# Attention followed by a gated MLP in fp32: the gelu's denominator made as |h|·(b1·|h| + b0) with its product on GpSimd, in place of a square on ScalarE and a sum on VectorE

## Chip, cores and metric

One core of a Trainium2 chip. The metric is the device time of one execution in microseconds (us): 651.39 us, the median of three runs of the kernel before (651.1 to 655.28). Engines are named as in the profile: PE (TensorE matmul), PEld (TensorE weight load), DVE (VectorE), ACT (ScalarE), POOL (GpSimd), SP (SyncE, which here issues DMAs).

## The reference, cut to what matters

Local attention (4 batches, 8 heads, 768 positions, head size 64, a window of 16 keys to either side and 24 block summaries) makes `x` of 3072 tokens by 512. Then comes the part that the change touches:

```python
h = x @ w_in                      # 3072 x 2048
h2 = h * h
h3 = h2 * h
P = a[0] + a[1] * h + a[2] * h2 + a[3] * h3
Q = 1.0 + np.abs(b[0]) * np.abs(h) + np.abs(b[1]) * h2
g = P / (Q + 1e-06)
return (g @ w_out).astype(np.float32)
```

All of it is fp32. The weights arrive as 8-byte floats. `Q` is the denominator of which the change speaks.

## The kernel before, in words

**Tiling.** The 3072 tokens are six groups of 512 (`GT`); the 2048 hidden columns are 16 tiles of 128 (`NFC`). One step is one group and one tile, so there are 96 steps, and the loop at L551 runs them in order, with `LAG` = 3 more turns for what trails. fp32 precision is kept by splitting each operand of a matmul into a high and a low part. In each step `moe1` (L390) makes `h`, 128x512, in PSUM from 12 matmuls (high·high, low·high, high·low, four chunks each), `gelu` (L402) turns `h` into `gh` and `gl`, and three steps later `moe2` (L432) adds 12 matmuls with `gh` and `gl` into four PSUM tiles `po`.

**The gelu** (L402 to L430) has these instructions for each step, all 128x512. ACT: a square, an absolute value with scale, a linear form `tu`. DVE: `tq` = square·b1 + |h|·b0 (L420). ACT: `ta` = exp(-ln(`tq` + 1)), the reciprocal. DVE: two products that finish the cubic `P` in `tu` (L407, L409), then `gh`, a remainder in `tq`, a remainder in `tu` (L426 to L428). POOL: `gl` = `tu`·`ta` (L430). `ta`, `tq` and `tu` have two buffers each, `h` two PSUM buffers, `gh` and `gl` three. The square goes either into `tq` itself, in SBUF, or into a PSUM tile `sq` of the pool `ps_a`, which attention uses too (L413 to L415). The first form is taken in steps 0, 1, 3, 4, 6, 7, 9 and 10, in later steps that start attention, and from the end of attention on; the second in the rest.

**What else runs.** Attention works in halves of 64 positions. A half's scores come from PE (`sc`); DVE adds the mask and takes the extreme (`ss`, a custom instruction, and `sm`); ACT makes the exponentials; DVE the reciprocal of their sum; POOL scales the four parts of `ss` (L245); then PE transposes (`pt`) and multiplies with the values (`av`). During the first 14 steps the weights are also split (`w_split`, L353): for each of the 16 tiles ACT scales the raw words `wr`, POOL makes integers of a byte of each (L369), DVE joins them (L372), ACT rounds the high part into `wearly` or `w` (L382) and DVE subtracts for the low part (L385).

**Order.** PE's order is that of the program text throughout. For the first 14 steps (`NSTRICT`) the orders of DVE, ACT and POOL are too: the string `STEP` (L56) lists what each step issues, `g0` being the next part of this step's gelu and `g1` that of the step before. After that the scheduler of the tile framework orders DVE, ACT and POOL by priority and by its own estimate of times. Every engine runs its queue in order, so an instruction that waits holds back all behind it on that engine.

The constants sit in `cs`: columns 4 and 5 hold |b0| and |b1| scaled by 2^-32, column 7 the scaled 1.000001.

Of the kernel before, what the change touches and what calls it, by code (L numbers as in the profile page):

```python
# [8 lines left out]
F32 = mybir.dt.float32  # L9
# [3 lines left out]
AF = mybir.ActivationFunctionType  # L13
ALU = mybir.AluOpType
# [8 lines left out]
P = 128  # L23
NPAIR = H // 2
NCC = DM // P
NFC = DFF // P
# [8 lines left out]
GT = 512  # L35
# [18 lines left out]
NSTRICT = NFC - 2  # L54
CROSS = 1
STEP = "h3 k0 h0 l0 h1 a0 w2 h1 g1 h3 h0 u w3 g0 w2 g0 q0 h0 w2 g1 w3 q0 P2 v h2 g0"  # L56
NHALF = NT // HQ
# [3 lines left out]
def tile_kernel(ctx, tc, qw_in, kraw, kwin, vpad, vred, wio, a, b, cmask, cident, cavg, out):  # L61
# [12 lines left out]
    ps_a = ctx.enter_context(tc.tile_pool(name="ps_a", bufs=2, space=PSUM))  # L74
# [23 lines left out]
    pe, dve, act, gps = Kept(nc.tensor), Kept(nc.vector), Kept(nc.scalar), Kept(nc.gpsimd)  # L98
# [6 lines left out]
    cs = const.tile([P, 8], F32, name="cs")  # L105
# [13 lines left out]
    def setup():  # L119
        nc.scalar.dma_start(out=mask, in_=cmask)  # L120
        nc.scalar.dma_start(out=ident, in_=cident)
        nc.scalar.dma_start(out=coef[:, 0:4], in_=a)
        nc.scalar.dma_start(out=coef[:, 4:6], in_=b)
        dve.tensor_scalar_mul(cs[:, 0:6], coef, SH)
        dve.tensor_scalar_mul(cs[:, 6:7], cs[:, 5:6], -1.0)
        dve.tensor_tensor(cs[:, 5:6], cs[:, 5:6], cs[:, 6:7], op=ALU.max)
        dve.memset(cs[:, 7:8], C1 * SH)

    ksum, vsum, att, x32, prods = {}, {}, {}, {}, {}
# [272 lines left out]
    def gelu(h, gh, gl, g, fc):  # L402
        ta = mp.tile([P, GT], F32, tag="ta", name=f"ta{g}_{fc}")
        tq = mp.tile([P, GT], F32, tag="tq", name=f"tq{g}_{fc}")
        tu = mp.tile([P, GT], F32, tag="tu", name=f"tu{g}_{fc}")
        def products():
            dve.tensor_tensor(tu, tu, h, op=ALU.mult)  # L407
            yield
            dve.scalar_tensor_tensor(out=tu, in0=tu, scalar=cs[:, 1:2], in1=h, op0=ALU.add, op1=ALU.mult)  # L409


        prods[g * NFC + fc] = products()
        sq = tq  # L413
        if g * NFC + fc < start_of(NHALF - 1) + 4 and ((g * NFC + fc) not in halves if g * NFC + fc > NSTRICT else g * NFC + fc in (2,5,8,11,12,13,)):
            sq = ps_a.tile([P, GT], F32, tag="a", name=f"sq{g}_{fc}")  # L415
        act.activation(sq, h, AF.Square)
        act.activation(ta, h, AF.Abs, scale=cs[:, 4:5])
        act.activation(tu, h, AF.Identity, scale=cs[:, 3:4], bias=cs[:, 2:3])
        yield
        dve.scalar_tensor_tensor(out=tq, in0=sq, scalar=cs[:, 5:6], in1=ta, op0=ALU.mult, op1=ALU.add)  # L420
        yield
        act.activation(ta, tq, AF.Ln, bias=cs[:, 7:8])
        act.activation(ta, ta, AF.Exp, scale=-1.0)
        yield
        lead(prods.pop(g * NFC + fc), True)
        dve.scalar_tensor_tensor(out=gh, in0=tu, scalar=cs[:, 0:1], in1=ta, op0=ALU.add, op1=ALU.mult)  # L426
        dve.scalar_tensor_tensor(out=tq, in0=tq, scalar=C1 * SH, in1=gh, op0=ALU.add, op1=ALU.mult)
        dve.scalar_tensor_tensor(out=tu, in0=tu, scalar=cs[:, 0:1], in1=tq, op0=ALU.add, op1=ALU.subtract)  # L428
        yield
        gps.tensor_tensor(gl, tu, ta, op=ALU.mult)  # L430
# [62 lines left out]
    def lead(chain, all_of=False):  # L493
        for _ in chain or ():
            if not all_of:
                return
# [37 lines left out]
    def start_of(jj):  # L534
        return EARLY_HALF[jj - HPG] if jj < 2 * HPG else NFC - 2 - (jj >= 3 * HPG) + 4 * ((jj - 2 * HPG) // 2)

    halves = {}
# [13 lines left out]
    for step in range(NG * NFC + LAG):  # L551
        g, fc = divmod(step, NFC)
# [133 lines left out]
```

## Time and profile before

| what | value |
|---|---|
| time, median of 3 runs | 651.39 us (651.1 to 655.28) |
| profiled execution, first to last instruction (span) | 647.9 us |
| busy: PE, DVE, ACT, POOL | 96%, 89%, 71%, 40% of the span |
| POOL `gl`, 96 instructions, mean | 1345 ns |
| POOL waited for DVE's `tu` | 159.6 us |
| ACT waited for DVE's `tq` | 74.7 us |

The page gives the profiled execution's span and no time of its own beside it; the median of the runs is 3.49 us above the span, for what lies before the first and after the last instruction. A row of a group reads: line, engine, operation, output<-inputs, shapes, count, then busy us and mean ns of one, then the idle time before. Every line is L88 here because one helper records all operations, so groups are told apart by tile names. In a table of windows each engine has its busy us and the number of its instructions. A row of a timeline has start, duration, engine, instruction, count, and in brackets the idle time before it with what ended it.

### The profile page before, as it was taken

Reading aid. Unit: us, or ns where it says so; the run is one execution under the profiler, and the core shown is the slowest. Engines: PE = TensorE matmul, PEld = TensorE weight load, DVE = VectorE, ACT = ScalarE, POOL = GpSimd, SP = SyncE. Lnnn points to the kernel's source line nnn. Section 1 sums busy time; section 2 is a strip of 40 time slices with the busy share of each in tenths; the row PEclk is TensorE's granted clock in tenths of the full one; section 3 lists DMA queues with packets and bytes.
Section 4 is the critical chain, followed back from the end, with each engine's and each line's share of the span. In section 5 each row is a group of like instructions: output and inputs, shape, how many; then the busy total and the mean of one; then the engine's idle time right before and its main releaser. Section 6 shows DMA issues by size and latency. Waiting matters only on the chain.

```text
span 647.9 us, 11828 instructions
## 1 busy us (share of the span) xinstructions
PE 624.7 (96%) x4068; PEld 499.4 (77%) x4068; DVE 576.9 (89%) x1152; ACT 459.0 (71%) x1032; POOL 257.4 (40%) x350
## 2 busy tenths in 40 slices
PE   8998879988999999999999999999999999999997
PEld 5666657866788887788888778888788888888886
DVE  4699999999998989988999999988988888988885
ACT  3889869977677577767758677758767756765652
POOL 1855666754243235244233244333334232222221
PEclk9999979989999999999999999999999999999999
DMA  9997644403354435234424332314233110010001
GB/s 322 340 356 263 205 148 157 139 26 107 113 176 116 125 122 160 83 128 150 119 88 141 103 129 93 108 63 130 66 129 114 40 64 1 21 45 1 0 2 65
DMA packets 51559, 77.00 MB, mean 119 GB/s; under 512 B 6068, under 2 KB 33076, under 8 KB 49580
## 3 DMA queue, kind: packets, MB, share of 16 engines
q1 hardware_dynamic: 50796, 75.80, 36.1%
q8 instruction: 32, 0.52, 0.3%
q10 hardware_dynamic: 576, 0.25, 0.1%
q0 software_dynamic: 128, 0.20, 0.1%
q14 instruction: 27, 0.22, 0.1%
HBM read 61.31 MB, written 14.73 MB: 117 GB/s over the span
## 4 chain that ended last, share of the span: by engine, by line
PE 51%; DVE 29%; ACT 7%; issue 6%; POOL 6%; DMA 1%; SPq 0%; DVEq 0%; POOLq 0%
PE po L88 24%; PE h L88 22%; DVE tu L88 10%; DVE tq L88 7%; DVE gh L88 4%; POOL ss L88 4%; ACT ss L88 3%; PE av L88 2%; DVE xl L88 2%; PE sc L88 2%; ACT ta L88 2%; DVE ss L88 2%; DVE ks L88 1%; DMA kres<-in_kraw_dram 1%; PE pt L88 1%
## 5 line engine op out<-in xcount | busy, mean ns | idle before, releaser
L88 POOL TENSOR_TENSOR gl<-tu,ta 128x512 fp32r<-128x512 f32 x96 | 129.1, 1345 | 298.9 <-DVE tu L88 159.6
L88 POOL TENSOR_SCALAR ss<-ss,sm 128x120 f32<-128x120 f32 x192 | 95.2, 513 | 81.6 <-DVE sm L88 79.5
L88 ACT ACTIVATE ta<-tq,cs 128x512 f32<-128x512 f32 x96 | 69.7, 726 | 76.3 <-DVE tq L88 74.7
L88 PE MATMUL po<-wearly,gh 128*128 128x512 f32 x384 | 122.8, 401 | 0.0
L88 PE MATMUL po<-w,gh 128*128 128x512 f32 x384 | 121.7, 398 | 0.0
L88 PE MATMUL h<-xh,wearly 128*128 128x512 f32 x384 | 96.1, 392 | 1.6 <-DVE sm L88 1.1
L88 PE MATMUL h<-xh,w 128*128 128x512 f32 x384 | 95.0, 389 | 0.0
L88 PEld LDWEIGHTS h<-xh,wearly 128*128 128x128 f32 x384 | 71.9, 188 | 18.7 <-ACT wr L88 1.3
L88 ACT ACTIVATE ss<-ss,sm 128x120 f32<-128x120 f32 x192 | 73.2, 384 | 15.4 <-DVE sm L88 15.2
L88 PEld LDWEIGHTS h<-xh,w 128*128 128x128 f32 x384 | 72.0, 188 | 15.2 <-ACT x L88 0.2
L88 PEld LDWEIGHTS po<-w,gh 128*128 128x128 f32 x384 | 71.3, 190 | 16.0 <-issue 1.7
L88 PEld LDWEIGHTS po<-wearly,gh 128*128 128x128 f32 x384 | 70.6, 191 | 16.2 <-issue 2.2
L88 DVE SCALAR_TENSOR_TENSOR gh<-tu,cs,ta 128x512 fp32r<-128x512 f32 x96 | 73.2, 762 | 9.2 <-ACT ta L88 1.2
L88 PE MATMUL po<-w,gl 128*128 128x512 f32 x192 | 75.4, 393 | 0.0
L88 PE MATMUL po<-wearly,gl 128*128 128x512 f32 x192 | 75.4, 393 | 0.0
L88 DVE SCALAR_TENSOR_TENSOR tu<-tu,cs,tq 128x512 f32<-128x512 f32 x96 | 72.9, 760 | 2.5
L88 ACT ACTIVATE tu<-h,cs 128x512 f32<-128x512 f32 x96 | 74.7, 778 | 0.0
L88 DVE SCALAR_TENSOR_TENSOR tu<-tu,cs,h 128x512 f32<-128x512 f32 x96 | 71.3, 743 | 2.3
L88 DVE SCALAR_TENSOR_TENSOR tq<-tq,gh 128x512 f32<-128x512 f32 x96 | 66.3, 691 | 3.0
L88 ACT ACTIVATE ta<-h,cs 128x512 f32<-128x512 f32 x96 | 65.2, 679 | 3.0 <-POOL gl L88 2.9
L88 DVE TENSOR_TENSOR tu<-tu,h 128x512 f32<-128x512 f32 x96 | 64.9, 676 | 0.0
L88 ACT ACTIVATE ta<-ta 128x512 f32<-128x512 f32 x96 | 60.9, 634 | 2.8
(73 smaller groups left out, 925.3 us busy)
## 6 DMA issues: line engine op xcount, KB each, us to landing
wr<-in_wio_dram SPq DMA_DIRECT2D x15, 1024.0 KB
cross<-tb SPq DMA_DIRECT2D x32, 256.0 KB
vw<-in_vpad_dram SPq DMA_DIRECT2D x42, 192.0 KB
kw<-in_kwin_dram SPq DMA_DIRECT2D x40, 192.0 KB
pts<-cross SPq DMA_DIRECT2D x96, 64.0 KB
out_dram<-o SPq DMA_DIRECT2D x24, 256.0 KB
qw<-in_qw_dram SPq DMA_DIRECT2D x40, 128.0 KB
kr<-in_kraw_dram SPq DMA_DIRECT2D x12, 384.0 KB
```

The source lines that it names most:

```text
L88: out = getattr(self.engine, name)(*args, **kw)
```

## The change

The denominator without its constant, b1·h² + b0·|h|, is computed as |h|·(b1·|h| + b0). ACT makes |h| without a scale into `ta`; ACT reads `ta` and makes b1·|h| + b0 into `tq`; POOL multiplies the two into `tq`. The square, the PSUM tile `sq` with its rule, and the DVE instruction go. In the set-up one DVE instruction makes |b0| and |b1| together, where two made |b1| alone.

```diff
-        dve.tensor_scalar_mul(cs[:, 6:7], cs[:, 5:6], -1.0)
-        dve.tensor_tensor(cs[:, 5:6], cs[:, 5:6], cs[:, 6:7], op=ALU.max)
+        dve.scalar_tensor_tensor(out=cs[:, 4:6], in0=cs[:, 4:6], scalar=-1.0, in1=cs[:, 4:6], op0=ALU.mult, op1=ALU.max)
...
         prods[g * NFC + fc] = products()
-        sq = tq
-        if g * NFC + fc < start_of(NHALF - 1) + 4 and ((g * NFC + fc) not in halves if g * NFC + fc > NSTRICT else g * NFC + fc in (2,5,8,11,12,13,)):
-            sq = ps_a.tile([P, GT], F32, tag="a", name=f"sq{g}_{fc}")
-        act.activation(sq, h, AF.Square)
-        act.activation(ta, h, AF.Abs, scale=cs[:, 4:5])
+        act.activation(ta, h, AF.Abs)
+        act.activation(tq, ta, AF.Identity, scale=cs[:, 5:6], bias=cs[:, 4:5])
         act.activation(tu, h, AF.Identity, scale=cs[:, 3:4], bias=cs[:, 2:3])
         yield
-        dve.scalar_tensor_tensor(out=tq, in0=sq, scalar=cs[:, 5:6], in1=ta, op0=ALU.mult, op1=ALU.add)
+        gps.tensor_tensor(tq, tq, ta, op=ALU.mult)
         yield
         act.activation(ta, tq, AF.Ln, bias=cs[:, 7:8])
         act.activation(ta, ta, AF.Exp, scale=-1.0)
```

How this moves instructions: PE's order is the same in both. DVE, ACT and POOL change in the three places below. In the rows a name such as `gl0_7` is `gl` of group 0, step 7, `ss13` is attention's half 13, `wr11` the raw weights of tile 11, and the number after the last underscore is an instance number of the listing.

POOL in steps 8 and 9 of the first group, where the text sets the order; before:

```order
L88 TENSOR_SCALAR ss13_1194<-ss13_1194,sm13_1195 128x120 x4
L88 TENSOR_TENSOR gl0_7_1160<-tu0_7_1203,ta0_7_1201 128x512
L88 TENSOR_SCALAR wr11_1030<-wr11_1030 128x1024
L88 TENSOR_TENSOR gl0_8_1249<-tu0_8_1262,ta0_8_1260 128x512
L88 TENSOR_SCALAR wr12_1216<-wr12_1216 128x1024
```

and with the change:

```order
L88 TENSOR_SCALAR ss13_1191<-ss13_1191,sm13_1192 128x120 x4
L88 TENSOR_TENSOR tq0_8_1258<-tq0_8_1258,ta0_8_1257 128x512
L88 TENSOR_TENSOR gl0_7_1157<-tu0_7_1200,ta0_7_1198 128x512
L88 TENSOR_SCALAR wr11_1027<-wr11_1027 128x1024
L88 TENSOR_TENSOR tq0_9_1343<-tq0_9_1343,ta0_9_1342 128x512
L88 TENSOR_TENSOR gl0_8_1246<-tu0_8_1259,ta0_8_1257 128x512
L88 TENSOR_SCALAR wr12_1213<-wr12_1213 128x1024
```

The new product of a step stands ahead of `gl` of the step before and of the weights' conversion `wr`.

DVE over the same stretch; before:

```order
L88 SCALAR_TENSOR_TENSOR gh0_7_1159<-tu0_7_1203,cs_95,ta0_7_1201 128x512
L88 SCALAR_TENSOR_TENSOR tq0_7_1202<-tq0_7_1202,gh0_7_1159 128x512
L88 SCALAR_TENSOR_TENSOR tu0_7_1203<-tu0_7_1203,cs_95,tq0_7_1202 128x512
L88 SCALAR_TENSOR_TENSOR tq0_8_1261<-sq0_8_1263,cs_95,ta0_8_1260 128x512
L88 TENSOR_TENSOR tu0_8_1262<-tu0_8_1262,h0_8_1235 128x512
L88 TENSOR_TENSOR w10_1267<-wr10_975,w10_1267 128x1024
L88 SCALAR_TENSOR_TENSOR tu0_8_1262<-tu0_8_1262,cs_95,h0_8_1235 128x512
L88 SCALAR_TENSOR_TENSOR wr11_1030<-wr11_1030 128x1024
```

and with the change:

```order
L88 SCALAR_TENSOR_TENSOR gh0_7_1156<-tu0_7_1200,cs_95,ta0_7_1198 128x512
L88 SCALAR_TENSOR_TENSOR tq0_7_1199<-tq0_7_1199,gh0_7_1156 128x512
L88 SCALAR_TENSOR_TENSOR tu0_7_1200<-tu0_7_1200,cs_95,tq0_7_1199 128x512
L88 TENSOR_TENSOR tu0_8_1259<-tu0_8_1259,h0_8_1232 128x512
L88 TENSOR_TENSOR w10_1263<-wr10_973,w10_1263 128x1024
L88 SCALAR_TENSOR_TENSOR tu0_8_1259<-tu0_8_1259,cs_95,h0_8_1232 128x512
L88 SCALAR_TENSOR_TENSOR wr11_1027<-wr11_1027 128x1024
```

One row is gone and nothing else moved; the last row needs POOL's `wr11`.

ACT in steps 7 and 8 of the second group, where the scheduler sets the order; before:

```order
L88 ACTIVATE sq1_7_2357<-h1_7_2339 128x512
L88 ACTIVATE ta1_7_2354<-h1_7_2339,cs_95 128x512
L88 ACTIVATE tu1_7_2356<-h1_7_2339,cs_95 128x512
L88 ACTIVATE ta1_7_2354<-tq1_7_2355,cs_95 128x512
L88 ACTIVATE ta1_7_2354<-ta1_7_2354 128x512
L88 ACTIVATE sq1_8_2418<-h1_8_2400 128x512
L88 ACTIVATE ta1_8_2415<-h1_8_2400,cs_95 128x512
```

and with the change:

```order
L88 ACTIVATE ta1_7_2341<-h1_7_2326 128x512
L88 ACTIVATE tu1_7_2343<-h1_7_2326,cs_95 128x512
L88 ACTIVATE tq1_7_2342<-ta1_7_2341,cs_95 128x512
L88 ACTIVATE ta1_8_2401<-h1_8_2386 128x512
L88 ACTIVATE tu1_8_2403<-h1_8_2386,cs_95 128x512
L88 ACTIVATE tq1_8_2402<-ta1_8_2401,cs_95 128x512
L88 ACTIVATE ta1_7_2341<-tq1_7_2342,cs_95 128x512
L88 ACTIVATE ta1_7_2341<-ta1_7_2341 128x512
```

The affine form now comes third, after `tu`, and here the logarithm of step 7 stands behind three instructions that need `h` of step 8.

## The prediction, made before the changed kernel was run

> **What bounds the kernel now.** I read the table of windows first, because the shares of the whole span mix two regimes.
>
> ```profile
> 37.00:135.00 98.00, 88.03 (x550) 66.47 (x551) 95.17 (x177) 86.50 (x178) 62.10 (x55) 0.96 0.58 193
> 135.00:183.00 48.00, 45.06 (x287) 35.78 (x287) 45.88 (x94) 34.77 (x84) 17.28 (x21) 0.98 0.32 98
> 183.00:530.00 347.00, 343.94 (x2266) 280.98 (x2265) 313.91 (x659) 247.23 (x579) 128.90 (x210) 1.00 0.36 111
> 530.00:633.00 103.00, 103.00 (x482) 85.14 (x481) 90.30 (x117) 63.53 (x102) 26.27 (x19) 1.00 0.03 11
> ```
>
> The columns after the window's length are PE, PEld, DVE, ACT and POOL busy, then the granted clock and DMA. From 183 to 633 us PE is busy for 446.94 of 450 us: DVE could be free there and little would change, since the most that can be won is 3 us. From 37 to 135 us it is otherwise: PE is busy for 88.03 of 98 us, DVE for 95.17. Here DVE sets the pace, and this is where the change can give or cost. The two rows of the same windows for the instructions on `h` alone count the steps: 156 matmuls, 13 steps of 12, in the first, and 84, seven steps, in the second.
>
> ```profile
> 37.00:135.00 98.00, 38.83 (x156) 29.06 (x156) 16.94 (x24) 23.08 (x38) 0.96 0.58 193
> 135.00:183.00 48.00, 20.75 (x84) 15.77 (x84) 9.92 (x14) 12.33 (x21) 0.98 0.32 98
> ```
>
> Next, one early step on POOL and on DVE, step 8 of group 0 (from one DVE `wr` to the next, 103.25 to 110.60, 7.35 us).
>
> ```profile
> 103.42 3.77 POOL L88 TENSOR_SCALAR ss<-ss,sm 128x120 f32<-128x120 f32 x4 [1.91 <-DVE sm L88]
> 107.16 1.30 POOL L88 TENSOR_TENSOR gl<-tu,ta 128x512 fp32r<-128x512 f32 x1
> 108.55 2.01 POOL L88 TENSOR_SCALAR wr<-wr 128x1024 int32<-128x1024 uint8 x1
> ...
> 103.25 1.19 DVE L88 SCALAR_TENSOR_TENSOR wr<-wr 128x1024 int32<-128x1024 int32 x1
> 104.36 0.74 DVE L88 SCALAR_TENSOR_TENSOR gh<-tu,cs,ta 128x512 fp32r<-128x512 f32 x1
> 105.14 0.69 DVE L88 SCALAR_TENSOR_TENSOR tq<-tq,gh 128x512 f32<-128x512 f32 x1
> 105.87 0.75 DVE L88 SCALAR_TENSOR_TENSOR tu<-tu,cs,tq 128x512 f32<-128x512 f32 x1
> 106.53 0.75 DVE L88 SCALAR_TENSOR_TENSOR tq<-sq,cs,ta 128x512 f32<-128x512 f32 x1
> 107.20 0.68 DVE L88 TENSOR_TENSOR tu<-tu,h 128x512 f32<-128x512 f32 x1
> 108.08 1.46 DVE L88 TENSOR_TENSOR w<-wr,w 128x1024 fp32r<-128x1024 f32 x1 [0.21 <-ACT w L88]
> 109.47 0.73 DVE L88 SCALAR_TENSOR_TENSOR tu<-tu,cs,h 128x512 f32<-128x512 f32 x1
> 110.60 1.23 DVE L88 SCALAR_TENSOR_TENSOR wr<-wr 128x1024 int32<-128x1024 int32 x1 [0.39 <-POOL wr L88]
> ```
>
> Two things are to be seen. The last row waits for POOL's `wr`: in this step POOL's queue, not DVE, ends the wait. And POOL is slow because it takes turns with DVE: its four small scalings need 3.77 us while DVE runs `wr`, `gh`, `tq`, `tu`, all with two inputs in SBUF, and POOL's `wr` takes 2.01 us, of which 1.02 come after DVE's `w` has ended at 109.54. Steps 9 and 10 end the other way round, with POOL ahead:
>
> ```profile
> 114.17 1.29 POOL L88 TENSOR_TENSOR gl<-tu,ta 128x512 fp32r<-128x512 f32 x1 [3.61 <-DVE tu L88]
> ...
> 114.72 1.29 DVE L88 SCALAR_TENSOR_TENSOR tq<-tq,cs,ta 128x512 f32<-128x512 f32 x1
> 115.94 0.68 DVE L88 TENSOR_TENSOR tu<-tu,h 128x512 f32<-128x512 f32 x1
> 118.74 1.19 DVE L88 SCALAR_TENSOR_TENSOR wr<-wr 128x1024 int32<-128x1024 int32 x1
> ```
>
> ```profile
> 118.92 3.76 POOL L88 TENSOR_SCALAR ss<-ss,sm 128x120 f32<-128x120 f32 x4 [1.91 <-PE sc L88]
> 122.65 1.29 POOL L88 TENSOR_TENSOR gl<-tu,ta 128x512 fp32r<-128x512 f32 x1
> 124.03 1.45 POOL L88 TENSOR_SCALAR wr<-wr 128x1024 int32<-128x1024 uint8 x1
> ...
> 122.83 1.65 DVE L88 SCALAR_TENSOR_TENSOR tq<-tq,cs,ta 128x512 f32<-128x512 f32 x1
> 124.41 0.68 DVE L88 TENSOR_TENSOR tu<-tu,h 128x512 f32<-128x512 f32 x1
> 127.22 1.19 DVE L88 SCALAR_TENSOR_TENSOR wr<-wr 128x1024 int32<-128x1024 int32 x1
> ```
>
> Step 9 has no scalings on POOL and takes 118.74 - 110.60 = 8.14 us; step 10 takes 127.22 - 118.74 = 8.48. In both the instruction that the change removes, `tq<-tq,cs,ta`, started while `gl` ran and took until `gl` was done.
>
> **The change part by part.** The groups give the prices.
>
> ```profile
> L88 POOL TENSOR_TENSOR gl<-tu,ta 128x512 fp32r<-128x512 f32 x96 | 129.1, 1345 | 298.9 <-DVE tu L88 159.6 <-ACT ta L88 70.3 <-DVE sm L88 27.2
> L88 DVE SCALAR_TENSOR_TENSOR tq<-tq,cs,ta 128x512 f32<-128x512 f32 x43 | 48.1, 1118 | 11.3 <-ACT ta L88 10.9
> L88 DVE SCALAR_TENSOR_TENSOR tq<-sq,cs,ta 128x512 f32<-128x512 f32 x53 | 39.1, 738 | 4.0 <-ACT ta L88 3.9
> L88 ACT ACTIVATE sq<-h 128x512 f32<-128x512 f32 x53 | 30.9, 583 | 27.3 <-PE h L88 27.3
> L88 ACT ACTIVATE ta<-tq,cs 128x512 f32<-128x512 f32 x96 | 69.7, 726 | 76.3 <-DVE tq L88 74.7
> L88 ACT ACTIVATE ta<-ta 128x512 f32<-128x512 f32 x96 | 60.9, 634 | 2.8
> ```
>
> Removed from DVE: 48.1 + 39.1 = 87.2 us. Added to POOL: 96 products of two SBUF operands of 128x512, the kind of `gl`, so 96 x 1.345 = 129 us. On ACT a 583 ns square becomes an affine form read from SBUF, between the 634 and the 726 ns of the two such rows: 5 to 14 us in all, hidden in ACT's 99.77 idle us of 183 to 530; in the early window 13 times 0.05 to 0.14 lie in 11.5 idle us. The set-up loses one small DVE instruction, and some DMA issues on SP move by a place or two; both I take as nothing, for the constants are made before the first `h`, and no row above waits for those transfers.
>
> The same DVE operation costs 738 ns with its first input in PSUM and 1118 ns with both in SBUF: 380 ns are waiting for POOL. The Trainium skill, page "SBUF — State Buffer", section "Who interferes with whom", says so as a rule: a DVE instruction with two SBUF inputs and a GpSimd instruction that reads SBUF exclude each other, and the second to issue is blocked until the first is done. The trace agrees in kind (the 1.65 us above), and the rule speaks against this change; what it would make of the sum is a rival below.
>
> *Steps 0 to 13.* Step 8 after the change: scalings done at 3.91 us (107.16 - 103.25), the new product 1.30, DVE's `w` in its turn 1.2, `gl` 1.30, `wr` 1.02, and only then DVE's next `wr`: 8.73 us instead of 7.35, +1.38. The cover that DVE gives up (0.75) is worth nothing here, because POOL's queue ends the step. Behind the product stand `gl` and `wr`, and DVE's `wr` and so `gh` wait for the latter. Step 9: DVE loses 1.22 (115.94 - 114.72); the product takes its turn once among `gh`, `tq`, `tu`, and holds one up by up to 1.30: +0.1. Step 10: the same POOL sum as step 8, 8.73, against 8.48: +0.25. Together +1.7 for three steps. The three kinds recur, so four rounds in steps 2 to 13: **+6.9 us**. Bounds: if DVE never waits for the new product, step 8 is 3.91 + 1.30 + 1.30 + 1.02 = 7.53 (+0.2), step 9 loses 1.2, step 10 is bound by the same 7.53 (-0.95): -1.95 a round, -7.8. If in every step the product comes on top with nothing in return, 1.35 to 1.38 each, 4.1 a round: +16.4. I take the value in between because the rows show turns being taken.
>
> *Steps 13 to 19, 135 to 183 us.* DVE is busy for 45.88 of 48 us, POOL for 17.28 only. Seven steps lose 0.74 each, -5.2. The three two-input instructions of a step (0.74, 0.69, 0.75) fill about a third of its 6.9 us, so I charge a third of 1.3 back, 0.4 each: **-2.4 us**, bounds -5.2 and, with 1.3 each, +3.9.
>
> *183 to 633 us.* What hides the longer way is the lag of three steps:
>
> ```profile
> 581.49 2.72 PE h L88 x12
> 600.52 2.72 PE po L88 x12
> 633.16 10.95 PE po L88 x48
> ...
> 590.58 1.29 POOL L88 TENSOR_TENSOR gl<-tu,ta 128x512 fp32r<-128x512 f32 x1 [4.50 <-DVE tu L88]
> 640.22 1.29 POOL L88 TENSOR_TENSOR gl<-tu,ta 128x512 fp32r<-128x512 f32 x1 [4.50 <-DVE tu L88]
> ```
>
> `h` of a step is done at 584.21, its `gl` at 591.87, and PE reads it from 600.52 on: 8.65 us to spare. The affine form behind `tu` (0.7), a product of 1.3 instead of 0.74, and `gl` behind the next step's product (1.3) use about 2.6 of it. **0 us**, bounds -3 (all of PE's idle time) and +8 (the ACT rival). Without that cover the 2.6 us would come in every step.
>
> *The end.* Only the last step has no cover: its `gl` ends at 641.51 and PE's last matmuls need it. One more 0.7 on ACT and 0.56 on POOL, against DVE's old wait for the `gl` before: **+0.2**, bounds 0 and 1.3.
>
> Sum: 6.9 - 2.4 + 0 + 0.2 = +4.7 us on the span of 647.9, so 652.6. The median of the runs, 651.39, is 3.49 above the span; the forecast is **656.1 us**, 0.7% slower, which a measurement of this kernel, good to about 1%, may not tell from no change.
>
> **The rivals.** *The freed DVE wins.* Two DVE waits go, 0.74 to 1.2 us a step, and no new ones come. For it: DVE is busy for 95.17 of 98 us. Against it: POOL ends step 8, and the new work stands in that very queue. By the lower bounds -7.8 - 5.2 = -13.0: 638.4 us. It would need steps 9 and 10 shorter by over 1 us each. Chance 0.12.
>
> *The shared port fills up, slower.* Place: steps 2 to 13, between POOL's product and DVE's `gh`, `tq`, `tu`, `w`. Price: each of the steps pays the product whole, +16.4 - 2.4 + 0.2: 665.6 us. It decides for "slower" as soon as steps 9 and 10 grow by over 0.5 each. For it: the 3.77 us of the scalings; against it: the removed SBUF form gives the port back 0.74 in two of three steps. Chance 0.26. This is the rule of the Trainium skill's page "SBUF — State Buffer" taken at its word, every overlap blocked for the whole instruction.
>
> *ACT's new order costs PE in the attention steps, slower.* In the order of the second group the logarithm of step 7 stands behind three instructions that wait for `h` of step 8, one PE step of 5.44 us (twice 2.72) later. With the 2.6 from above 0.6 of the 8.65 are left. If attention's work on ACT eats that and 0.5 us is lost in each of the 14 rounds of four steps (96 steps less the 20 counted above and the 19 that 103 us hold at 5.44), +7: 663.1 us. Against it: gaps of that kind would have to pass the two buffers of `ta` without the scheduler's other work filling them. Chance 0.14.
>
> *Within 1%*, the forecast, has 0.48. Faster by over 1% is the first rival, 0.12; slower by over 1% the two others, 0.40. The forecast's own range is 651 to 658. The range for 8 in 10 goes from 645, half of the first rival's gain, to 667, past the port rival.
>
> **What would show it.** Right: in step 8 and the two like it (three steps before and after) DVE's wait for POOL's `wr` grows from 0.39 to over 1 us, and those steps last 8.5 to 8.8; the new product takes about 1.3 us; from 37 to 135 us DVE's busy share falls while the work of that window takes 5 to 8 us longer; PE stays above 99% from about 190 us on. Wrong: the thirteenth step done earlier than before; `gh`, `tq` and `tu` keeping 0.69 to 0.75 while POOL's product runs; PE idle by more than 6 us in the attention steps after 190; or a product far from 1.3 us.

## The result, and the profile after

The changed kernel takes **687.02 us** (median of 4 runs, 686.13 to 690.64) against 651.77 us for the kernel before beside it: a ratio of 1.0556, 95% interval 1.0513 to 1.0599, 35 us slower. The forecast was 656.1 us, 0.7% slower, with a range from 645 to 667. The change is slower, and by more than any case of the prediction allowed (665.6 us at most). Of all runs of the kernel before, one took 693.0 us at a granted clock of 0.85, where every other run shows 0.93 or more; it is left out of the medians and ratios below.

First the same windows as in the prediction's table, up to 530 us (PE, PEld, DVE, ACT and POOL busy, granted clock, DMA):

```profile
37.00:135.00 98.00, 85.64 (x546) 65.05 (x546) 87.67 (x163) 84.96 (x171) 78.88 (x65) 0.97 0.57 191
135.00:183.00 48.00, 41.17 (x261) 30.73 (x260) 41.17 (x65) 32.18 (x65) 29.25 (x28) 0.96 0.23 69
183.00:530.00 347.00, 323.22 (x2101) 263.62 (x2098) 277.46 (x575) 234.67 (x555) 189.37 (x244) 0.99 0.35 109
```

The third row is the news: PE, which had been busy for 343.94 of 347 us, is idle there for 23.8. DVE, from which the work was taken, got emptier in every row, and PE did not gain from it in any.

The early steps look as they were forecast. POOL, then DVE, in the place that the prediction's step 8 had:

```profile
109.16 1.28 POOL L88 TENSOR_TENSOR tq<-tq,ta 128x512 f32<-128x512 f32 x1
110.41 2.27 POOL L88 TENSOR_TENSOR gl<-tu,ta 128x512 fp32r<-128x512 f32 x1
...
105.40 1.23 DVE L88 SCALAR_TENSOR_TENSOR wr<-wr 128x1024 int32<-128x1024 int32 x1 [0.30 <-POOL wr L88]
109.50 2.02 DVE L88 TENSOR_TENSOR w<-wr,w 128x1024 fp32r<-128x1024 f32 x1
113.91 1.23 DVE L88 SCALAR_TENSOR_TENSOR wr<-wr 128x1024 int32<-128x1024 int32 x1 [1.73 <-POOL wr L88]
121.96 1.23 DVE L88 SCALAR_TENSOR_TENSOR wr<-wr 128x1024 int32<-128x1024 int32 x1 [0.31 <-POOL wr L88]
```

From one DVE `wr` to the next, step 8 takes 113.91 - 105.40 = 8.51 us (7.35 before), and DVE's wait for POOL's `wr` has grown from 0.39 to 1.73; step 9 takes 8.05 (8.14). The steps like 8, three steps before and after it, take 8.46 and 8.52 us where they had 7.26 and 7.32. `gl` and `w` hold each other up: 2.27 us and 2.02 us, where they had 1.30 and 1.46.

The groups after show the product's price and what else became longer:

```profile
L88 POOL TENSOR_TENSOR tq<-tq,ta 128x512 f32<-128x512 f32 x96 | 129.2, 1346 | 125.3 <-ACT tq L88 125.0
L88 DVE SCALAR_TENSOR_TENSOR gh<-tu,cs,ta 128x512 fp32r<-128x512 f32 x96 | 91.0, 948 | 40.1 <-ACT ta L88 38.6 <-ACT tq L88 0.5
L88 DVE SCALAR_TENSOR_TENSOR tq<-tq,gh 128x512 f32<-128x512 f32 x96 | 78.4, 817 | 7.2
L88 ACT ACTIVATE tq<-ta,cs 128x512 f32<-128x512 f32 x96 | 77.9, 812 | 0.5
L88 ACT ACTIVATE ta<-h 128x512 f32<-128x512 f32 x96 | 57.0, 593 | 95.1 <-POOL gl L88 79.3 <-PE h L88 15.7
```

The product costs 1346 ns, as forecast. `gh` went from 762 to 948 ns and `tq<-tq,gh` from 691 to 817, without any edit to them. The last row is the one to remember: ACT's absolute value, the first instruction of a step's gelu, now waits 79.3 us for POOL's `gl`.

Who waits for whom from 183 to 530 us, before and then after (total us, times, longest):

```profile
ACT sq L88 <- PE h L88: 22.8, 26, 2.1
ACT tq L88 <- PE h L88: 13.6, 11, 2.1
PE av L88 <- DVE tu L88: 2.1, 4, 1.1
```

```profile
ACT ta L88 <- POOL gl L88: 54.4, 32, 4.6
ACT ta L88 <- POOL tq L88: 38.0, 28, 4.1
DVE tu L88 <- ACT tu L88: 24.1, 15, 3.2
PE av L88 <- DVE tu L88: 21.8, 13, 3.8
```

Before, ACT came to a new step early and waited for PE's `h` (22.8 + 13.6 us). After, ACT waits for POOL, DVE waits for ACT, and PE waits for DVE: 21.8 of PE's 23.8 idle us stand in one row. One such place after, and the same place before:

```profile
457.03 1.07 PE L88 MATMUL h<-xl,w 128*128 128x512 f32 x4
...
460.61 1.64 POOL L88 TENSOR_TENSOR gl<-tu,ta 128x512 fp32r<-128x512 f32 x1 [2.31 <-DVE tu L88]
461.21 1.58 DVE L88 SCALAR_TENSOR_TENSOR tq<-tq,gh 128x512 f32<-128x512 f32 x1
462.28 0.60 ACT L88 ACTIVATE ta<-h 128x512 f32<-128x512 f32 x1 [2.56 <-POOL gl L88]
464.37 0.75 DVE L88 SCALAR_TENSOR_TENSOR tu<-tu,cs,h 128x512 f32<-128x512 f32 x1
465.17 1.15 PE L88 MATMUL av<-pts,vw 120*64 120x64 f32 x32 [1.63 <-DVE tu L88]
```

```profile
435.48 1.07 PE L88 MATMUL h<-xl,w 128*128 128x512 f32 x4
436.47 1.15 PE L88 MATMUL av<-pts,vw 120*64 120x64 f32 x32
436.58 0.60 ACT L88 ACTIVATE tq<-h 128x512 f32<-128x512 f32 x1 [2.05 <-PE h L88]
```

Before, `h` is done at 436.55 and ACT starts on it at 436.58. After, an `h` done at 458.10 is first touched at 462.28, over 4 us later, and until DVE's second product has read it at 465.12 its PSUM buffer is not free. `av` needs that buffer: the pool of two that holds `h` holds `av` as well. So every fourth step, when attention's `av` comes, PE finds the pool full.

To see where along the program the time is lost, I took the start of ACT's 96 instructions `tu<-h,cs`, one a step, and subtracted the same step's start in the trace of before: +4.5 us at step 12, +8.4 at step 16, +8.1 at step 20, +23.3 at 48, +37.1 at 76, +36.4 at 95. The 29 us between steps 20 and 76 are 14 rounds of four steps, 2.1 us a round; after step 76, where attention ends, nothing more is lost. From step 20 to step 76 PE stands idle for 24.4 us (3.1 before) and is busy for 346.3 (338.6). So 21.3 of the 29.0 us are PE's waiting. In the other 7.7 PE is busy for longer, at a granted clock of 0.99 there against 1.00; what makes them up was not followed further.

The two traces lie 37.6 us apart, the medians 35.25, so these delays come out some 2 us larger than the difference of the medians. Every timed run lies 1.7 to 2.1 us above its own span; the 3.49 us of the prediction, between the span of 647.9 and the median, are therefore not all time outside the span.

### The profile page after: what moved, and what is told of

It is laid out like the page before. It is cut to its first block, busy times and chain, and to the rows that moved or that the text cites. A ratio compares the mean times of both kernels' runs of the same rounds, so it can differ in the third digit from the quotient of the medians.

```text
span 685.5 us, 11963 instructions
## 1 busy us (share of the span) xinstructions
PE 632.8 (92%) x4068; PEld 503.9 (74%) x4068; DVE 537.4 (78%) x1055; ACT 467.2 (68%) x1032; POOL 392.4 (57%) x446
## 4 chain that ended last, share of the span: by engine, by line
POOL 27%; DVE 24%; ACT 18%; PE 13%; issue 10%; DMA 1%; POOLq 0%; DVEq 0%; ACTq 0%
POOL gl L88 9%; POOL ss L88 8%; ACT ta L88 8%; POOL tq L88 8%; DVE tu L88 7%; DVE gh L88 6%; PE po L88 6%; DVE tq L88 5%; PE h L88 4%; ACT tu L88 3%; ACT ss L88 3%; ACT tq L88 3%; POOL wr L88 2%; DVE ss L88 2%; DVE xl L88 1%
## 5 line engine op out<-in xcount | busy, mean ns | idle before, releaser
L88 POOL TENSOR_TENSOR gl<-tu,ta 128x512 fp32r<-128x512 f32 x96 | 135.8, 1414 | 122.0 <-DVE tu L88 75.9
L88 POOL TENSOR_TENSOR tq<-tq,ta 128x512 f32<-128x512 f32 x96 | 129.2, 1346 | 125.3 <-ACT tq L88 125.0
L88 ACT ACTIVATE ta<-tq,cs 128x512 f32<-128x512 f32 x96 | 69.3, 722 | 78.5 <-POOL tq L88 78.1
L88 DVE SCALAR_TENSOR_TENSOR gh<-tu,cs,ta 128x512 fp32r<-128x512 f32 x96 | 91.0, 948 | 40.1 <-ACT ta L88 38.6
L88 ACT ACTIVATE ta<-h 128x512 f32<-128x512 f32 x96 | 57.0, 593 | 95.1 <-POOL gl L88 79.3
L88 POOL TENSOR_SCALAR ss<-ss,sm 128x120 f32<-128x120 f32 x192 | 97.7, 526 | 35.8 <-DVE sm L88 35.0
L88 PE MATMUL h<-xh,wearly 128*128 128x512 f32 x384 | 98.2, 397 | 4.3 <-ACT xh L88 2.5
L88 ACT ACTIVATE ss<-ss,sm 128x120 f32<-128x120 f32 x192 | 73.3, 384 | 21.9 <-DVE sm L88 21.4
L88 DVE SCALAR_TENSOR_TENSOR tq<-tq,gh 128x512 f32<-128x512 f32 x96 | 78.4, 817 | 7.2
L88 DVE SCALAR_TENSOR_TENSOR tu<-tu,cs,tq 128x512 f32<-128x512 f32 x96 | 80.5, 839 | 2.4
L88 ACT ACTIVATE tq<-ta,cs 128x512 f32<-128x512 f32 x96 | 77.9, 812 | 0.5
```

The costliest lines, as they stand in the source:

```text
L88: out = getattr(self.engine, name)(*args, **kw)
```

## The experiments

All are timed against the kernel before on the same chip; the difference is between the medians. The last column is PE's busy time in the window of 347 us from 183 to 530, from each run's profile (343.94 in the kernel before, 323.22 in the changed one); it is a rough guide, since the granted clock in that window lies between 0.97 and 1.00, and at 0.94 in dvepsum.

| kernel | us | ratio, 95% interval | difference | PE busy |
|---|---|---|---|---|
| early | 658.90 | 1.0094 (1.0060 to 1.0129) | +6.7 | 343.43 |
| late | 681.14 | 1.0458 (1.0389 to 1.0527) | +29.0 | 324.83 |
| ring3 | 685.99 | 1.0538 (1.0503 to 1.0573) | +34.6 | 326.47 |
| pad32 | 688.45 | 1.0569 (1.0532 to 1.0605) | +37.0 | 324.79 |
| dveprod | 681.94 | 1.0467 (1.0446 to 1.0487) | +30.5 | 326.66 |
| dvepsum | 668.77 | 1.0257 (1.0193 to 1.0320) | +16.6 | 336.73 |
| sqsbuf | 660.07 | 1.0118 (1.0062 to 1.0175) | +7.9 | 337.66 |
| load | 672.04 | 1.0325 (1.0291 to 1.0359) | +20.6 | 334.21 |
| loadlate | 666.67 | 1.0236 (1.0194 to 1.0278) | +15.7 | 334.32 |
| memset | 654.84 | 1.0054 (1.0020 to 1.0088) | +3.4 | 339.85 |
| hop | 664.83 | 1.0225 (1.0185 to 1.0265) | +13.7 | 334.84 |
| hopload | 699.35 | 1.0742 (1.0694 to 1.0789) | +48.4 | 321.56 |
| tulast | 688.29 | 1.0574 (1.0548 to 1.0600) | +36.9 | 319.26 |
| tulast3 | 693.41 | 1.0658 (1.0623 to 1.0693) | +42.0 | 321.36 |
| dvetul | 662.22 | 1.0176 (1.0149 to 1.0202) | +11.0 | 336.62 |
| ava | 703.80 | 1.0812 (1.0776 to 1.0849) | +52.6 | 320.67 |
| square | 637.29 | 0.9789 (0.9772 to 0.9806) | -14.1 | 346.81 |
| sqload | 657.38 | 1.0109 (1.0085 to 1.0134) | +6.2 | 344.18 |

They were run in five lots: ring3, pad32, dveprod and load; sqsbuf, dvepsum, early and late; tulast3, tulast, square and memset; hop, sqload, dvetul and ava; loadlate and hopload. Below they stand by question. The scheduler orders the later steps of each version by itself, so a version can differ from its neighbour in more than the lines shown.

**First thoughts: a ring of buffers, the shared SBUF, or ACT's order.** ACT's absolute value waits for `gl` because `ta` has two buffers. With three it need not. SBUF has no room for a third, so a padding tile was cut by 256 bytes a partition; pad32 has that cut alone.

```diff
-    const.tile([P, 96], F32, name="shift")
+    const.tile([P, 32], F32, name="shift")
...
-        ta = mp.tile([P, GT], F32, tag="ta", name=f"ta{g}_{fc}")
+        ta = mp.tile([P, GT], F32, tag="ta", name=f"ta{g}_{fc}", bufs=3)
...
```

> The changed kernel with three buffers of ta in place of two (a padding tile is 256 bytes smaller to make room). Theory 1, the buffer ring: from 183 us on ACT waits 79.3 us for gl before it may write |h| into ta, because gl of two steps before stands on POOL behind the next step's product; a third buffer takes that wait away, so the 29 us lost after 183 us go and some 8 lost before stay: 655 to 664 us, and the wait of ACT's ta for POOL's gl under 10 us. Theory 2, the shared port: the 37 us more of busy time in DVE's gh, tq and tu (250 us against 212) come from POOL's product whatever the buffers: 680 to 690 us. Theory 3, ACT's order (the logarithm of one step behind instructions that need the next h): the scheduler may order anew, 670 to 690.

> The changed kernel with only the padding tile 256 bytes smaller, the control for ring3. All theories: 687 us within 1%.

Neither moved the time by as much as 3 us. In the version with three buffers ACT's waits for `gl` shrink from 79.3 us to 10.6, and its waits for the product, at the logarithm, grow from 78.1 us in the changed kernel to 110.6:

```profile
ACT ta L88 <- POOL tq L88: 110.6, 76, 4.8
```

The two buffers are one place where the delay showed, not what made it. The first theory fell. Next, the product on DVE, with all else as changed:

```diff
-        gps.tensor_tensor(tq, tq, ta, op=ALU.mult)
+        dve.tensor_tensor(tq, tq, ta, op=ALU.mult)
```

> The changed kernel with the product |h|(b1|h| + b0) made by DVE in place of POOL. Theory 1, the ring: gl is no longer behind a product of 1.35 us on POOL, so the trip from |h| to gl is shorter by about 2 us, but ta is still written first: 652 to 662 us. Theory 2, the port: the extra 129 us of POOL reads go, DVE has 96 times 0.69 us, about as before: 650 to 655. Theory 3, ACT's three dependent instructions and their order: 675 to 690.

30.5 of the 35 us are still lost with no product on POOL at all: theories 1 and 2 fell, and the third named the range. And the reverse, POOL's work without the change: the kernel before, with one unused product of two slices of `gl` behind each `gl`.

```diff
...
         gps.tensor_tensor(gl, tu, ta, op=ALU.mult)
+        gps.tensor_tensor(spare, gl[:, 0:GT - 64].bitcast(F32), gl[:, 64:GT].bitcast(F32), op=ALU.mult)
```

> The kernel before with one more POOL product of 128x448 in each step, right behind gl, whose inputs are gl and whose output nobody reads. It loads POOL and the port as the change does, by some 1.15 us a step, but no engine waits for it and ACT's order stays that of before. Theory 1, the ring: only the first 14 steps lose, where POOL ends some steps: 655 to 664 us. Theory 2, the port: 675 to 690 us.

20.6 us, between the ranges of both theories. So each half alone costs more than half of the loss: more than one thing is at work, and the parts do not add.

**Where it is lost.** The new form in some steps and the old one in the others.

```diff
+        if g * NFC + fc < NSTRICT:
+            act.activation(ta, h, AF.Abs)
...
+        else:
+            sq = tq
...
+            act.activation(sq, h, AF.Square)
...
```

This is early; late has >= in place of <. `NSTRICT` is 14, and behind the else stands the whole old form, with the square in PSUM in the same steps as before.

> The new form of the denominator in steps 0 to 13 alone, the old form with its square in PSUM in the 82 later steps. By the delays read from the two traces (4.5 us at step 12, 8.4 at step 16) it costs 4 to 9 us: 655 to 661 us, whatever the cause. If the late loss were only the consequence of the early steps' disorder (buffers that come free later), it would come here too: 675 to 688 us.

> The old form in steps 0 to 13, the new form with POOL's product in steps 14 to 95. If the loss grows locally, in the steps that hold the new form, 675 to 682 us, that is 24 to 31 over the kernel before, and with the kernel that has it in the early steps alone it adds up to the whole loss of 35. If the lag of three steps hides the longer way after 183 us, as the prediction had it, and the loss comes out of the early part, 651 to 657 us.

+6.7 and +29.0 add up to 35.7, about the 35 us of the whole. The early part of the prediction stands; 29.0 us come from steps that it had costed at nothing, or at a small gain in the first few, and they are not an after-effect of the early ones.

**Which half of the edit.** Before the change 53 squares went into PSUM; in the changed form nothing of the denominator does. sqsbuf is the kernel before with all squares in SBUF (the rule of L414 taken out). dvepsum is dveprod with the affine form in PSUM in those 53 steps; `s` is `tq` or, by the old rule, that PSUM tile:

```diff
...
-        act.activation(tq, ta, AF.Identity, scale=cs[:, 5:6], bias=cs[:, 4:5])
+        act.activation(s, ta, AF.Identity, scale=cs[:, 5:6], bias=cs[:, 4:5])
...
-        dve.tensor_tensor(tq, tq, ta, op=ALU.mult)
+        dve.tensor_tensor(tq, s, ta, op=ALU.mult)
```

> The kernel before, with one edit: ACT writes the square into SBUF in all 96 steps, where 53 of them had it in PSUM. DVE still makes the denominator, ACT's three instructions on h keep their order. Theory SBUF sharing (a DVE instruction with two SBUF inputs and a POOL instruction hold each other up; the change lost time because the PSUM form is gone and because a product came to POOL): 53 sums go from 738 towards the 1118 ns of the 43 others, and the kernel comes most of the way to the 681.9 us of the version with the product on DVE, 668 to 682 us. Theory ACT's order (what costs is that the affine form is read from SBUF behind the absolute value, and so the chain to the logarithm is longer): nothing of that is in this kernel, 650 to 656 us.

> The changed kernel with the product on DVE, and the affine form written into PSUM in the same 53 steps in which the square had been there. Theory SBUF sharing: 53 products have one SBUF input again and pay about 0.74 us, so nearly all of the 30 us comes back, 651 to 660 us. Theory ACT's order: the absolute value, the affine form behind it and the product stand as in the version with the product on DVE, 678 to 684 us.

Neither theory got its numbers: the place of the square is worth 7.9 us, not 17 to 30, and PSUM gives back 14 of dveprod's 30 us, not all and not none.

**What POOL's work costs by itself.** memset puts three memsets of the same 448 columns in the place of load's unused product: about as long on POOL's queue, kept behind `gl` in its order, but nothing read.

```diff
...
-        gps.tensor_tensor(gl, tu, ta, op=ALU.mult)
+        made = gps.tensor_tensor(gl, tu, ta, op=ALU.mult)
+        for _ in range(3):
+            idle = gps.memset(spare, 0.0)
+            tc.add_manual_dep(idle.ins, made.ins.name, ORDERED, reason="order of the text")
```

> The kernel before with three memsets of 128x448 on POOL behind each gl: about as much time on POOL's queue as the unused product had, which cost 20.6 us (672.0 against 651.4), but no reading of SBUF. Theory SBUF sharing: DVE's operations keep 0.69 to 0.75 us, 651 to 656 us. If the queue itself is what costs (gl and the scalings behind other work on POOL), 665 to 675 us.

3.4 us against 20.6. The rows of load and of memset side by side:

```profile
L88 POOL TENSOR_TENSOR spare<-gl 128x448 f32<-128x448 f32 x96 | 123.5, 1287 | 6.3
L88 DVE SCALAR_TENSOR_TENSOR gh<-tu,cs,ta 128x512 fp32r<-128x512 f32 x96 | 95.6, 996 | 9.4 <-ACT ta L88 1.5 <-ACT ss L88 0.5
```

```profile
L88 POOL MEMSET spare<- 128x448 f32 x288 | 136.3, 473 | 9.7
L88 DVE SCALAR_TENSOR_TENSOR gh<-tu,cs,ta 128x512 fp32r<-128x512 f32 x96 | 73.5, 766 | 9.4 <-ACT ta L88 2.4
```

The memsets keep POOL busy for 136.3 us and the product for 123.5, yet DVE's `gh` takes 766 ns beside the former (762 in the kernel before) and 996 beside the latter. What lengthens `gh` is not POOL's time but POOL's reading. The Trainium skill, page "SBUF — State Buffer", section "Who interferes with whom", states just that: a DVE instruction with two SBUF inputs contends with a GpSimd instruction that reads SBUF and not with one that only writes it. The two rows agree with it.

**What the trip through POOL costs by itself.** hop is the kernel before with one tiny POOL instruction from step 14 on. It reads 8 columns; all it does is to put POOL's queue between DVE's sum and ACT's logarithm.

```diff
+        if g * NFC + fc >= NSTRICT:
+            gps.tensor_scalar(tq[:, 0:8], tq[:, 0:8], 1.0, 0.0, op0=ALU.mult, op1=ALU.add)
         act.activation(ta, tq, AF.Ln, bias=cs[:, 7:8])
```

> The kernel before, and from step 14 on one tiny POOL instruction more a step: it copies 8 columns of the denominator onto themselves between DVE's sum and ACT's ln, so that ln waits for a place in POOL's queue, while POOL reads next to nothing of SBUF. Theory (a), the trip through a second in-order queue: ln comes late whenever gl or the attention's scalings stand ahead of the tiny instruction, and as ACT works in order abs, tu and so DVE's products come late as well: 660 to 675 us. Theory (b), sharing of SBUF alone: 651 to 656 us.

13.7 us, inside the range of theory (a), from 27.1 us of POOL work:

```profile
L88 POOL TENSOR_SCALAR tq<-tq 128x8 f32<-128x8 f32 x82 | 27.1, 330 | 123.6 <-DVE tq L88 123.6
...
L88 DVE SCALAR_TENSOR_TENSOR gh<-tu,cs,ta 128x512 fp32r<-128x512 f32 x96 | 74.3, 774 | 40.9 <-ACT ta L88 35.3 <-ACT sm L88 1.4 <-PE po L88 0.3
```

```profile
ACT ta L88 <- POOL tq L88: 80.2, 47, 3.7
PE av L88 <- DVE tu L88: 12.1, 7, 3.0
ACT sq L88 <- PE h L88: 8.2, 6, 3.1
```

```profile
459.78 2.75 POOL L88 TENSOR_SCALAR ss<-ss,sm 128x120 f32<-128x120 f32 x8
462.50 0.20 POOL L88 TENSOR_SCALAR tq<-tq 128x8 f32<-128x8 f32 x1
...
462.73 0.72 ACT L88 ACTIVATE ta<-tq,cs 128x512 f32<-128x512 f32 x1 [3.27 <-POOL tq L88]
```

DVE's instructions keep their length (774 ns), and still the picture of the changed kernel is there (183 to 530 us): ACT waits for POOL, no longer for PE (8.2 us where it had 22.8), and PE waits for DVE's products ahead of `av`, 12.1 us. In the rows of one place the tiny instruction stands behind eight of attention's scalings, and ACT's logarithm behind it waits 3.27 us. That is the second mechanism: ln, exp, abs and the linear form stand in one in-order queue, so the wait for POOL at the logarithm of one step makes `h` of the next be read late. What the two do together:

> The kernel before with the unused POOL product of 128x448 behind gl from step 14 on alone. By the delays of the run that has it in all steps (12.7 us at step 16, 25.9 at the end) the late steps pay 13: 661 to 667 us. If the late delay there was only the after-effect of the early steps: 651 to 656 us.

> The kernel before with both from step 14 on: the tiny POOL instruction between DVE's sum and ln, and the unused POOL product. DVE still makes the sum and the square still lies in PSUM. If the trip and the shared SBUF make up the late loss of the change, the time is near the 681.1 us of the kernel that has the change from step 14 on: 674 to 684 us. If the two overlap, the larger of them counts and it is 664 to 671 us; then the change's loss needs a third cause, such as ACT's affine form behind abs.

15.7 for the unused product in the late steps, 13.7 for the trip, **48.4 for both**, where their sum is 29.4. I had expected the sum at most, 684 us as the upper end, and rows of hopload show what I had not thought of:

```profile
458.69 1.29 POOL L88 TENSOR_TENSOR gl<-tu,ta 128x512 fp32r<-128x512 f32 x1 [2.86 <-PE po L88]
459.95 0.19 POOL L88 TENSOR_SCALAR tq<-tq 128x8 f32<-128x8 f32 x1
...
464.10 1.65 POOL L88 TENSOR_TENSOR gl<-tu,ta 128x512 fp32r<-128x512 f32 x1 [2.84 <-DVE tu L88]
...
460.17 0.72 ACT L88 ACTIVATE ta<-tq,cs 128x512 f32<-128x512 f32 x1 [2.28 <-POOL tq L88]
```

The tiny instruction of a step goes right behind `gl` of an earlier one, without a gap, because `gl` stands ahead of it in the queue. So the logarithm of one step, at 460.17, waits for the end of the gelu of another: steps that a lag was to keep apart run one behind the other, here at 5.41 us from `gl` to `gl`, as long as PE's two halves of a step (5.44), with nothing over for attention. In the changed kernel a product, too, starts right behind such a `gl`:

```profile
463.75 1.27 POOL L88 TENSOR_TENSOR gl<-tu,ta 128x512 fp32r<-128x512 f32 x1 [1.51 <-DVE tu L88]
464.99 1.27 POOL L88 TENSOR_TENSOR tq<-tq,ta 128x512 f32<-128x512 f32 x1
```

Both parts are in the changed kernel, and together they can cost more than its 29.0 us. That they make up just these 29.0 is argued, not shown, because hopload's queues stand in another order too. Among the gelu's instructions on ACT, the logarithm comes right behind `tu` 66 times in its trace, 94 times in the kernel before and 90 times in hop. And hopload goes on losing behind attention, where the changed kernel does not: there two steps take 11.72 us (`gl` at 645.00 and at 656.72), where PE's work for them is 10.88.

**The other side: no trip at all.** square makes the denominator on ACT alone. b1·|h|² + b0·|h| is a square, (r·|h| + c)² with r = sqrt(b1) and c = b0/(2r), less the constant c²; the constant goes into the logarithm's bias and into the scalar of DVE's remainder, so the kernel computes the same function with other roundings (it needs b1 other than zero). The set-up of these constants is left out here.

```diff
...
-        act.activation(ta, h, AF.Abs)
-        act.activation(tq, ta, AF.Identity, scale=cs[:, 5:6], bias=cs[:, 4:5])
+        act.activation(tq, h, AF.Abs)
+        act.activation(tq, tq, AF.Square, scale=cs[:, 6:7], bias=cs[:, 4:5])
...
-        gps.tensor_tensor(tq, tq, ta, op=ALU.mult)
...
-        dve.scalar_tensor_tensor(out=tq, in0=tq, scalar=C1 * SH, in1=gh, op0=ALU.add, op1=ALU.mult)
+        dve.scalar_tensor_tensor(out=tq, in0=tq, scalar=cs[:, 7:8], in1=gh, op0=ALU.add, op1=ALU.mult)
```

> The denominator made by ACT alone: abs, then the square of an affine form of it (the square is completed; the constant that is left over goes into the logarithm's bias and DVE's scalar), no product on POOL and none on DVE. It gives the same function with other roundings. Theory round trip: ln waits for ACT's own work only, about 3.4 us a step, so PE keeps its pace after 183 us and DVE's 87 us are really freed: 636 to 650 us. Theory SBUF sharing: no product on POOL, 53 sums less in SBUF, also 636 to 650 us. If instead the abs that waits for gl at the head of ACT's queue is the cause by itself, it stays: 665 to 685 us.

**637.29 us**, faster than both kernels: 0.9789 of the kernel before (0.9772 to 0.9806). The windows and groups:

```profile
37.00:135.00 98.00, 92.81 (x595) 70.73 (x596) 91.39 (x171) 93.31 (x185) 66.61 (x58) 0.98 0.58 194
183.00:530.00 347.00, 346.81 (x2311) 284.72 (x2310) 279.78 (x600) 253.69 (x579) 125.77 (x202) 1.00 0.34 107
...
L88 ACT ACTIVATE tq<-h 128x512 f32<-128x512 f32 x96 | 57.3, 597 | 119.6 <-PE h L88 117.1 <-DVE tu L88 2.5
L88 ACT ACTIVATE ta<-tq,cs 128x512 f32<-128x512 f32 x96 | 69.9, 728 | 2.0
```

The logarithm, which had waited 74.7 us for DVE, waits for nothing, and ACT is back in front of PE: it waits 117.1 us for `h`. PE is busy for 346.81 of 347 us, and the early window, where DVE set the pace, does more (595 matmuls against 550). By the same measure as above it gains 8.2 us up to step 16 and 4.4 more from there to the end. Freeing DVE does gain time when nothing new comes to POOL.

sqload puts load's unused product into this version:

> The version in which ACT makes the denominator alone (637.3 us), plus the unused POOL product of 128x448 behind every gl, which cost the kernel before 20.6 us. Theory (b): it costs about the same here, 652 to 662 us. Theory (a): SBUF sharing hurts most where it delays an operation that ACT's queue waits for, and here none stands between abs and ln: 638 to 648 us.

20.3 us more than square (+6.2 against -14.1), the price that theory (b) named. But the place is another:

```profile
183.00:530.00 347.00, 344.18 (x2319) 281.12 (x2320) 306.41 (x617) 256.56 (x596) 193.58 (x267) 1.00 0.37 114
...
L88 DVE SCALAR_TENSOR_TENSOR gh<-tu,cs,ta 128x512 fp32r<-128x512 f32 x96 | 102.0, 1063 | 21.9 <-ACT ta L88 13.4 <-ACT ss L88 1.4 <-PE po L88 1.1
```

`gh` is at 1063 ns, the longest of all runs that I list, and PE is busy for 344.18 of 347. By the delays of ACT's `tu`, sqload stands 17.8 us behind square at step 16 (3.7 of them before the first step) and 21.4 at step 95, so 3.6 us are lost in the steps after 16; load, in the kernel before, goes from 12.7 to 25.9 there. In both versions sharing SBUF costs time in the early steps; in the attention steps it cost much only in the one where ACT's logarithm waits for DVE. That the waiting is the reason is argued from these two runs.

**ACT's order.** In the late steps the scheduler put `tu` between the absolute value and the affine form. From step 14 on the affine form was put first, in ring3, in the changed kernel, and in dveprod:

```diff
-        act.activation(tq, ta, AF.Identity, scale=cs[:, 5:6], bias=cs[:, 4:5])
-        act.activation(tu, h, AF.Identity, scale=cs[:, 3:4], bias=cs[:, 2:3])
+        affine = act.activation(tq, ta, AF.Identity, scale=cs[:, 5:6], bias=cs[:, 4:5])
+        line = act.activation(tu, h, AF.Identity, scale=cs[:, 3:4], bias=cs[:, 2:3])
+        if g * NFC + fc >= NSTRICT:
+            tc.add_manual_dep(line.ins, affine.ins.name, ORDERED, reason="order of the text")
```

> The version with three buffers of ta, and one edit in ACT's order from step 14 on: the affine form of the denominator (tq) is put ahead of that of the numerator (tu), which stood between the absolute value and it. Nothing else moves, POOL's product is there in full. New theory, a round trip inside ACT's own queue: ACT runs ln, exp, abs, tu, tq and then stands idle for POOL's product before the next ln; in the version with three buffers this takes 4.96 us a step (ln at 457.82, 462.78, 467.74, 472.69) and leaves too little of PE's 5.44 for attention's work on ACT. With tq first, tu (0.77 us) runs beside the product and the trip takes about 4.3 us: 655 to 672 us. Theory SBUF sharing alone: POOL's product and DVE's three operations meet as before, 683 to 688 us.

> The same order on ACT, but with the two buffers of ta of the changed kernel. Theory round trip: the trip is shorter by about 0.65 us, but abs now waits for gl of two steps before, a second trip that runs over POOL and DVE and is shortened by the same 0.65 in two steps only: part of the gain, 662 to 682 us. Theory SBUF sharing alone: 685 to 689 us.

> The version with the product on DVE (681.9 us), and from step 14 on the affine form tq ahead of tu in ACT's queue. There the product started only after abs, tu and tq, and DVE had taken the first product of the numerator before it. Theory (a): the trip ACT, DVE, ACT of 5.73 us a step (ln at 451.64 and 457.37) becomes shorter than PE's 5.44: 660 to 674 us. Theory (b): the product stays a two-input SBUF operation that runs into gl: 679 to 684 us.

With the product on POOL this brought nothing (688.3 against 687.0), and with three buffers 693.4 instead of 686.0, above both ranges; 5.2 us of that are there in the trace before the first `tu`, where the edit does not reach but POOL's order changed too. With the product on DVE it brought 19.5 us (+11.0 instead of +30.5). ACT's rows there, dveprod and then dvetul:

```profile
454.07 0.81 ACT L88 ACTIVATE tq<-ta,cs 128x512 f32<-128x512 f32 x1
457.37 0.72 ACT L88 ACTIVATE ta<-tq,cs 128x512 f32<-128x512 f32 x1 [2.49 <-DVE tq L88]
```

```profile
450.19 0.81 ACT L88 ACTIVATE tq<-ta,cs 128x512 f32<-128x512 f32 x1
...
452.37 0.72 ACT L88 ACTIVATE ta<-tq,cs 128x512 f32<-128x512 f32 x1 [0.22 <-DVE tq L88]
```

From the affine form to the logarithm 3.30 us, of which ACT stands still for 2.49, become 2.18 with 0.22. So the length of the trip counts, as the theory says, but shortening it on ACT's side did not help where POOL is the other end. Why is not settled; what changed in tulast's rows is that DVE's `tq<-tq,gh` and `tu<-tu,cs,tq` became longer again (863 and 923 ns, against 817 and 839).

**The PSUM pool.** Last, `av` in the two buffers that the square had left:

```diff
-        av = ps_h.tile([P, NPAIR, 2, HQ], F32, tag="h", name=f"av{j0}")
+        av = ps_a.tile([P, NPAIR, 2, HQ], F32, tag="a", name=f"av{j0}")
```

> The changed kernel with the value products av in the PSUM buffers that the square had, in place of the two that h has. Theory (c): PE's waits for DVE's second product ahead of av (24.0 us in 15 waits) go, and h of the next steps no longer queues behind av: 664 to 676 us. Theories (a) and (b): the gelu's loop over ACT, POOL and DVE is as long as before and PE waits for it at another place: 682 to 690 us.

703.8 us, worse by 17 and outside both ranges. PE's waits for DVE's product ahead of `av` are gone, and PE waits ahead of the next scores instead, for ACT's copy of `av` in the same pool:

```profile
PE sc L88 <- ACT x L88: 27.1, 14, 3.8
```

The pool is the place where ACT's delay reaches PE, as the ring of `ta` is the place where POOL's reaches ACT. Moving the place did not shorten the delay.

## Why the prediction was wrong, point by point

*The early steps, +6.9 for steps 0 to 13 and -2.4 for 13 to 19:* together +4.5; the kernel that has the change there alone measures +6.7. The working holds: the steps like 8 take 8.46 to 8.52 us (8.73 forecast), step 9 8.05 (8.24), DVE's wait is 1.73 (over 1). One reading was loose: the sum `tq<-tq,cs,ta` did not end with `gl`, as the prediction says of steps 9 and 10, but 0.55 and 0.54 us after it (116.01 against 115.46, 124.48 against 123.94). The split was off: 4.5 us are lost by step 12 and, where 2.4 were to be won back, another 3.9 by step 16, which is the upper bound that the prediction gave for that stretch.

*183 to 633 us, 0:* **this is the step that failed.** "What hides the longer way is the lag of three steps: ... 8.65 us to spare." The lag does hide `gl` from PE: from 183 to 530 us the list of PE's waits has three rows, the 21.8 us ahead of `av` and two of about 1 us ahead of `h`, and none for `gl`. From step 20 to 75 `gl` is still done 3.9 us or more ahead of the matmuls that read it, in all but two steps (2.7 and 0.1). But the lag covers only the way from `h` to the matmuls that read its gelu. It does not cover the way back, on which the gelu frees the PSUM buffer of `h`, nor ACT's queue, which comes to the next `h` only after the logarithm of the last. Both have two buffers and in-order engines, not three steps. The bound of +8, the price of the rival on ACT's order, started from the same 8.65 us and so missed the 29.0 us that the steps from 14 on cost.

*The rival "ACT's new order costs PE in the attention steps"* named the place, at 0.14 and with 0.5 us a round. Measured are 2.1 us a round. Its mechanism was half of it: hop has ACT's order nearly as before and still loses 13.7 us, by a wait of ACT's queue for POOL's. With the product on DVE, ACT's order was worth 19.5 us; with the product on POOL, nothing.

*The rival "the shared port fills up"* had a mechanism that the runs show, in the wrong stage. It looked at steps 2 to 13 alone and added 9.5 us there to the forecast's 6.9, which the +6.7 does not bear out; but loadlate loses 15.7 us to it in the later steps. *"The freed DVE wins"* did not happen here, and square shows that it was not the gain that was missing: 14.1 us, close to the 13.0 that this rival worked out, though only some 8 of them are won by step 19, where the rival had all of its gain.

*The prices:* the product, 1.3 us forecast, 1346 ns; ACT's extra 5 to 14 us, 8.2 measured (459.0 to 467.2 us busy). That the latter fits is in part luck: the affine form costs 812 ns, more than the forecast's 634 to 726, and the absolute value without its scale 593 instead of 679, which the forecast did not count. "Hidden in ACT's 99.77 idle us" was wrong in kind: idle time of an in-order engine is no cover when the instruction that waits stands at its head.

*The end, +0.2:* the delay is 36.4 us at step 95 and the span is 37.6 longer, so 1.2, near the upper bound of 1.3.

Of the prediction's four signs of being wrong one came true, and it is the decisive one: PE idle by more than 6 us in the attention steps (23.8 from 183 to 530 us). The other three did not. The early steps got longer, the product took its 1.3 us, and `gh`, `tq` and `tu` did not keep their 0.69 to 0.75 but had means of 948, 817 and 839 ns.

What stays open: why the affine form ahead of `tu` helps with the product on DVE and not on POOL, and how the 29.0 us divide between the trip, the shared SBUF and the scheduler's order in the changed kernel itself. No run takes one of the three out of it and leaves the other two as they were.

## What to carry to other kernels

A pipeline's lag hid latency here only for the reader at its end. For every engine on the way ask separately which buffers the late step holds and what stands behind the waiting instruction in the in-order queue. An engine with idle time is not a free place for an instruction in the middle of a chain: a POOL instruction of 0.33 us a step, between DVE's sum and ACT's logarithm, cost 13.7 us here, and an unused one that reads SBUF took DVE's `gh`, with its two SBUF inputs, from 762 to 996 ns. When DVE is to be relieved, look first for algebra that keeps the chain on the engine that starts and ends it; the completed square did so and won 2.1%.

## What the runs showed of the hardware

ACT's price for 128x512 rises with each scale or bias that is read per partition from `cs`. In SBUF: 634 ns with none and 726 with one (`ta<-ta` and `ta<-tq,cs` before, in the prediction's rows), 812 with both (`tq<-ta,cs` after). From PSUM the groups show the same: 593 with none (`ta<-h` after), 679 with one (`ta<-h,cs` before), 770 with both (`tu<-h,cs` after). That is about 90 ns for each. The instructions of a row differ in function; where the function is the same, the absolute value, 593 and 679, differ by as much. The price makes the affine form the dearest ACT instruction of the gelu, where the forecast had 634 to 726 for it.
